# Delta-rule attention followed by two feed-forward layers, on one core: a new timetable for the start of the first layer and another order of its second matrix product

## The chip, the cores and the metric

The program is one kernel on one NeuronCore of a Trainium2 chip. What counts is the device time of one execution in microseconds (us), the median of several runs. The kernel's engines are TensorE (PE, with its weight loads PEld), VectorE (DVE), ScalarE (ACT), GpSimd (POOL) and SyncE (SP, which issues most transfers). A tile framework records the program in the order in which the Python code runs and sets the semaphores; each engine works off its own instructions in that order.

## The reference

Three stages run one after the other. The attention is a recurrence over 768 steps for 4 x 8 heads of width 48; the first feed-forward layer has 2048 hidden columns and a leaky activation with one slope for each column; the second has 1536 and a gated activation. The weights come out of the set-up as float64, since float32 arrays are multiplied there by a numpy float64.

```python
k_n = k / (np.linalg.norm(k, axis=-1, keepdims=True) + 1e-06)
for t in range(S):                      # attention: q, k, v, beta, S = 768
    y[:, :, t] = np.einsum('bhd,bhde->bhe', q[:, :, t], state)
    v_old = np.einsum('bhde,bhd->bhe', state, kt)
    state = state + bt[:, :, :, None] * np.einsum('bhd,bhe->bhde', kt, vt - v_old)
...
h = x @ w_in                            # first layer: x is 3072 x 384, w_in 384 x 2048
g = np.maximum(h, 0.0) + alpha * np.minimum(h, 0.0)
x = g @ w_out                           # back to 3072 x 384
...
g = x @ w_gate                          # second layer: 384 x 1536
out = (g * (1.0 / (1.0 + np.exp(-g))) * (x @ w_val)) @ w_out
```

## The kernel before

**The work.** The attention goes in 24 chunks of 32 steps; 4 chunks make a window. For each window the chunk's triangular system is inverted: `pre_T` transposes k or q on TensorE, `pre_G` makes the products of the keys, and `lanes` (windows 1 to 5) or `lanes2` (window 0, by blocks) does the substitution, a long row of small VectorE instructions (lines 258 and 266) with a part of the columns on GpSimd. Its last steps turn the result over into the tile TT (line 208). For each chunk there follow `do_KS` (keys times state, then `v` minus that on VectorE), `do_QS`, `do_U` (TT times v), `do_S` (the new state), `do_Y` and `do_XT` (the output, transposed into `xh` and `xl`, the high and the low part of x).

The first layer goes over 12 blocks of 256 tokens (two chunks) and 16 hidden slices: `H1(n, j)` is nine matmuls of 256 columns (line 600), then ScalarE (lines 610, 611) and VectorE (line 613) make the activation `pn`; `H1_parts` splits it into a high part `gh[0]` (ScalarE, line 621) and a low part `gh[1]` (GpSimd, line 622); `O1(n, j)` is nine matmuls with both (line 633). The second layer (`H2`, `O2`, lines 692 and 721) goes over 8 blocks of 384 tokens and 12 slices.

**Weights.** A matrix is used as a high and a low part, three products for each. The float64 words of a slice are turned into float32 by ScalarE (line 519) and three VectorE instructions (lines 527, 529, 533) and split by ScalarE (540) and GpSimd or VectorE (541). The generator `conv` does this for the 32 slices of the first layer, three steps a slice and 97 in all; `go(conv, n)` runs n steps of it. For the second layer the 36 slices are converted early, stored, fetched again at the end of the first layer (`fetch_w2`) and split (`make_w2`); 32 of them take the places of the first layer's slices.

**What sets the order.** `prelude()` is written out by hand. Everything after it stands in a list of events, each with a due time u; the list is sorted by u and run. One u is one pair of H1 and O1: `H1(n, j)` is due at 16n + j, `O1(n, j)` 2.5 later. The events of a chunk are due from `base(c)` on, here 20 for chunk 4, 25.7 for chunk 5, otherwise 8(c - 2). The first substitution on this list, window 1 (chunks 4 to 7), is spread over u = 6.6 to 18.5, the remaining 55 steps of `conv` over u = -0.5 to 13.5. `E1` is 192, the u at which the first layer's H1 ends.

Of the kernel before, what the change touches and what calls it, by code (L numbers as in the profile page):

```python
# [24 lines left out]
def kernel(  # L25
# [33 lines left out]
    NK = DM // 128  # L59
# [33 lines left out]
    nat = [ap.tile([128, H, 2, 64], F32, name=f"nat{z}") for z in range(2)]  # L93
# [207 lines left out]
    LANES = 5 + C - 1 + 1  # L301
# [286 lines left out]
    PASSES = ((0, 0), (0, 1), (1, 0))  # L588
# [36 lines left out]
    def O1(n, j):  # L625
        if j == 0:
            o1_t[n] = ps_o1.tile([128, 2, 512], F32, name="o1", tag="o1")
        o = o1_t[n]
        w = w1[2 * j + 1]
        g = g1_t.pop((n, j))  # L630
        for dm in range(NK):
            for i, (a, b) in enumerate(PASSES):
                nc.tensor.matmul(  # L633
                    o[:, dm // 2, (dm % 2) * N1:(dm % 2) * N1 + N1],
                    w[:, a, dm * 128:dm * 128 + 128],
                    g[:, b],
                    start=(j == 0 and i == 0 and dm % 2 == 0),
                    stop=(j == J1 - 1 and i == 2),
                    skip_group_check=True,
                )  # L640
        if j == J1 - 1:
            xs = g1.tile([128, 2, NK, 128], F32, name="xs", tag="xs", bufs=1)
            nc.scalar.activation(
                out=xs[:, :, 0:2, :].rearrange("p c k t -> p k c t"),
                in_=o[:, 0].rearrange("p (k c t) -> p k c t", k=2, c=2),
                func=AF.Copy,
            )
            nc.vector.tensor_copy(xs[:, :, 2, :], o[:, 1, 0:N1].rearrange("p (c t) -> p c t", c=2))
            nc.sync.dma_start(out=x2d[n], in_=xs)
            o1_t.pop(n)  # L650
# [87 lines left out]


    events = []  # L740

    def at(u, fn, *args):
        events.append((u, len(events), fn, args))
# [35 lines left out]
    conv = all_w1()  # L779

    def go(g, n=1):
        for _ in range(n):
            next(g, None)
# [4 lines left out]
    def prelude():  # L788
# [21 lines left out]
        n = 0  # L810
# [15 lines left out]
        inv = lanes2(0, True)  # L826
        go(inv, 3)
        n = 0
# [19 lines left out]
        warm(6)  # L848
        go(inv, 7)
        go(inv)  # L850
        go(conv, 4)
        go(inv)
        go(conv, 3)
        do_QS(0)
        do_U(0)
        go(conv, 3)
        do_S(0)
        load_k2(1)
        load_v(2)
# [4 lines left out]
        do_Y(0)  # L864
        do_QS(1)
        do_U(1)
        go(conv, 3)
        do_XT(0)
        go(conv, 2)
        do_Y(1)  # L870
# [3 lines left out]
        load_w1(*range(24, 2 * J1))  # L874
        go(conv, 3)
        do_XT(1)
        go(conv, 3)
        go(inv)
        go(conv, 3)
        go(inv)  # L880
        for z in range(4):
            pre_T(1, "q", z // 2, z % 2, nat)
        go(conv, 3)

    def base(c):
        return {4: 20, 5: 25.7}.get(c, 8 * (c - 2))

    CONV_DONE, CONV_END = 42, 14.0
    CONV_N = 3 * 2 * J1 + 1 - CONV_DONE
    for i in range(CONV_N):  # L890
        at(-0.5 + i * CONV_END / CONV_N, go, conv)
# [1 line left out]
    for w in range(1, NWIN):  # L893
        P = base(4 * w) - 32
        if w == 1:
            for z in range(2):
                at(0.6 + z, pre_G, 2 + z, (1,))
            for z in range(4):
                at(2.6 + z, pre_G, 4 + z)
            l0, l1, n = 6.6, 18.5, LANES  # L900
        else:
            at(P - 5, load_nat, w, "k", nat)
            at(P - 1, load_beta, w)
            for z in range(4):
                at(P + 1.2 + z, pre_T, w, "k", z // 2, z % 2, nat)
            at(P + 4.5, load_nat, w, "q", nat)
            for z in range(4):
                at(P + 7.2 + z, pre_T, w, "q", z // 2, z % 2, nat)
            for z in range(4):
                at(P + 11.2 + z, pre_G, 4 * w + z)  # L910
            l0, l1, n = P + 15, P + 31.5, LANES
        box = {}

        def step(w=w, box=box):
            if "g" not in box:
                box["g"] = lanes(w, 10)
            next(box["g"], None)

        for z in range(n):
            at(l0 + (l1 - l0) * z / n, step)  # L920

    for c in range(2, NCH):
        u = base(c)
        if c > 2:
            at(u - 7, load_v, c)
            at(u - 1.3, load_k2, c)
        at(u - 1.5, scale_v, c)
        at(u + 0.3, do_KS, c)
        at(u + 0.35, do_QS, c)
        at(u + 2.3, do_U, c)  # L930
        at(u + 4.3, do_S, c)
        at(u + 4.35, do_Y, c)
        at(u + 6.3, do_XT, c)
    for n in range(NB1):
        for j in range(J1):
            at(16 * n + j, H1, n, j)
# [2 lines left out]
    if WIDE2:  # L939
# [6 lines left out]
        for i in range(NW2):  # L946
            u = 24 + i * 4.0
# [5 lines left out]
    E1 = 16 * NB1  # L953
# [13 lines left out]
    late = list(range(2 * J1, 3 * J2))  # L967
    early2 = list(range(0, min(2 * J1, 3 * J2)))
    for i in early2:
        at(E1 - 16 + 1 + i / 2, fetch_w2, i)  # L970
        at(E1 - 16 + 3.1 + i / 2, make_w2, i)
    for i in late:
        at(E1 - 16 + 3 + i / 2, fetch_w2, i)
        at(E1 - 16 + 5.1 + i / 2, make_w2, i)
    at(E1 + LA + 0.6, end1)
    for n in range(NB2):
        u = E1 + LA + 1 + J2 * n
# [4 lines left out]
            at(u + j + 1.5, O2, n, j)  # L982

    with tc.manual_schedule():
        prelude()
        for _, _, fn, args in sorted(events, key=lambda e: e[:2]):
            fn(*args)

# [29 lines left out]
```

## Time and profile before

| what | value |
|---|---|
| median of 3 runs | 1161.68 us (1161.34 to 1162.38) |
| the profiled execution, its own time | 1160.9 us |
| its span, first to last instruction | 1159.2 us |
| mean granted TensorE clock | 0.953 |
| busy: TensorE, VectorE, ScalarE, GpSimd | 93%, 54%, 39%, 29% |

Outside the span lie 1.7 us of the profiled execution, and the median of the runs is 0.8 us above it. The busy shares are means over stages: up to about 76 us the attention of two chunks and the conversion alone, up to 696 us the first layer with the attention beside it, then the second layer. TensorE's granted clock stands at one of two levels, 1.0 (2.4 GHz) or 0.5 (1.2 GHz); a number between them is a mean over both. A figure such as "x163" is a count of instructions.

### The profile page before, as it was taken

Reading aid. Unit: us, or ns where it says so; the run is one execution under the profiler, and the core shown is the slowest. Engines: PE = TensorE matmul, PEld = TensorE weight load, DVE = VectorE, ACT = ScalarE, POOL = GpSimd, SP = SyncE. Lnnn points to the kernel's source line nnn. Section 1 sums busy time; section 2 is a strip of 40 time slices with the busy share of each in tenths; the row PEclk is TensorE's granted clock in tenths of the full one; section 3 lists DMA queues with packets and bytes.
Section 4 is the critical chain, followed back from the end, with each engine's and each line's share of the span. In section 5 each row is a group of like instructions: output and inputs, shape, how many; then the busy total and the mean of one; then the engine's idle time right before and its main releaser. Section 6 shows DMA issues by size and latency. Waiting matters only on the chain.

```text
span 1159.2 us, 37229 instructions
## 1 busy us (share of the span) xinstructions
PE 1083.7 (93%) x16125; PEld 1048.2 (90%) x16125; DVE 621.3 (54%) x1308; ACT 446.7 (39%) x1158; POOL 338.8 (29%) x522
## 2 busy tenths in 40 slices
PE   6578789899999999999999989999999999999996
PEld 5468689889989998998999979999999999999996
DVE  5669963794497379449734364333333333333332
ACT  4346344345435444544454673222222222222221
POOL 4234742563283256327433361101010000101000
PEclk8569789899999999999999999999999999999998
DMA  9652021234234323422322252010101010100000
GB/s 220 193 188 44 2 69 41 74 85 125 57 89 109 82 73 85 124 59 71 91 65 77 76 171 68 1 41 1 42 1 41 1 42 3 39 11 32 12 10 21
DMA packets 140080, 76.44 MB, mean 66 GB/s; under 512 B 104000, under 2 KB 134624, under 8 KB 139916
## 3 DMA queue, kind: packets, MB, share of 16 engines
q1 hardware_dynamic: 139340, 73.45, 23.3%
q8 instruction: 126, 2.06, 0.7%
q0 software_dynamic: 576, 0.61, 0.2%
q14 instruction: 38, 0.31, 0.1%
HBM read 57.52 MB, written 16.52 MB: 64 GB/s over the span
## 4 chain that ended last, share of the span: by engine, by line
PE 64%; DVE 17%; issue 13%; POOL 3%; ACT 2%; DMA 1%; POOLq 0%; SPq 0%; DVEq 0%; ACTq 0%
PE gv L692 21%; PE o L633 12%; PE h L600 11%; PE o L721 10%; DVE tmp L258 3%; DVE pn L613 2%; DVE X L266 2%; POOL w L541 2%; PE pg L168 2%; DVE wf L533 2%; PE pst L445 2%; PE pt L149 1%; DVE wf L529 1%; PE pu L427 1%; PE py L466 1%
## 5 line engine op out<-in xcount | busy, mean ns | idle before, releaser
L692 PE MATMUL gv<-x2s,w 128*128 128x384 f32 x1728 | 317.6, 336 | 0.0
L692 PEld LDWEIGHTS gv<-x2s,w 128*128 128x128 f32 x1728 | 304.1, 188 | 0.0
L633 PE MATMUL o<-gh,w 128*128 128x256 f32 x1728 | 256.2, 292 | 17.9 <-POOL gh L622 10.2
L600 PE MATMUL h<-xh,w 128*128 128x256 f32 x1152 | 242.9, 287 | 7.8 <-ACT pn L611 5.3
L633 PEld LDWEIGHTS o<-gh,w 128*128 128x128 f32 x1728 | 222.2, 193 | 29.8 <-POOL gh L622 14.8
L622 POOL TENSOR_TENSOR gh<-pn,gh 128x256 fp32r<-128x256 f32 x192 | 152.4, 794 | 304.2 <-ACT gh L621 255.3
L613 DVE SCALAR_TENSOR_TENSOR pn<-pn,nalpha 128x256 f32<-128x256 f32 x192 | 105.9, 551 | 186.8 <-ACT pn L611 182.7
L600 PEld LDWEIGHTS h<-xh,w 128*128 128x128 f32 x1152 | 195.3, 194 | 10.3 <-ACT pn L611 6.0
L600 PE MATMUL h<-xl,w 128*128 128x256 f32 x576 | 164.5, 286 | 2.0 <-DVE xl L492 2.0
L721 PE MATMUL o<-w,us 128*128 128x384 f32 x864 | 165.3, 336 | 0.0
L721 PEld LDWEIGHTS o<-w,us 128*128 128x128 f32 x864 | 151.1, 188 | 0.0
L704 DVE TENSOR_TENSOR sg<-sg,gv 128x384 f32<-128x384 f32 x96 | 53.2, 554 | 175.9 <-ACT sg L702 175.9
L621 ACT ACTIVATE gh<-pn 128x256 fp32r<-128x256 f32 x192 | 80.0, 416 | 141.8 <-DVE pn L613 141.3
L677 POOL TENSOR_TENSOR x2s<-x2r,x2s 128x384 fp32r<-128x384 f32 x21 | 20.7, 1014 | 333.8 <-ACT x2s L675 333.8
L600 PEld LDWEIGHTS h<-xl,w 128*128 128x128 f32 x576 | 111.8, 194 | 2.6 <-DVE xl L492 2.6
L707 ACT ACTIVATE us<-u 128x384 fp32r<-128x384 f32 x96 | 50.5, 526 | 165.0 <-DVE u L705 165.0
L610 ACT ACTIVATE pn<-h 128x256 f32<-128x256 f32 x192 | 72.2, 376 | 105.9 <-PE h L600 104.4
L702 ACT ACTIVATE sg<-gv 128x384 f32<-128x384 f32 x96 | 47.1, 491 | 169.4 <-PE gv L692 169.4
L708 DVE TENSOR_TENSOR us<-u,us 128x384 fp32r<-128x384 f32 x96 | 53.7, 559 | 62.8 <-ACT us L707 62.8
L705 DVE TENSOR_TENSOR u<-sg,gv 128x384 f32<-128x384 f32 x96 | 53.2, 554 | 45.8 <-PE gv L692 45.6
L611 ACT ACTIVATE pn<-h 128x256 f32<-128x256 f32 x192 | 72.5, 378 | 0.0
L258 DVE TENSOR_TENSOR tmp<-L,X 128x31 f32<-128x31 f32 (+29 forms) x155 | 64.2, 414 | 1.4
(102 smaller groups left out, 1062.3 us busy)
## 6 DMA issues: line engine op xcount, KB each, us to landing
w<-in_moe_w_out_dram SPq DMA_DIRECT2D x28, 384.0 KB
w2d<-wf SPq DMA_DIRECT2D x36, 192.0 KB
wf<-w2d SPq DMA_DIRECT2D x36, 192.0 KB
w<-in_moe_w_in_dram SPq DMA_DIRECT2D x16, 384.0 KB
nat<-in_k_dram SPq DMA_DIRECT2D x24, 192.0 KB
k<-in_k_dram SPq DMA_DIRECT2D x96, 48.0 KB
x2d<-xs SPq DMA_DIRECT2D x12, 384.0 KB
w<-in_moe_w_gate_dram SPq DMA_DIRECT2D x12, 384.0 KB
```

The costliest lines, as they stand in the source:

```text
L258: eng.tensor_tensor(w, t.L[:, i + 1:C, i:i + 1].to_broadcast([128, n, m]), t.X[:, i:i + 1, c0:c0 + m].to_broadcast([128, n, m]), ALU.mult,)
L600: nc.tensor.matmul(ps[:, 0:N1], w[:, a, kk * 128:kk * 128 + 128], x[b][:, kk, :], start=(i == 0), stop=(i == 3 * NK - 1),)
L610: nc.scalar.activation(out=pn[:, 1], in_=hv, func=AF.Relu, scale=-1.0)
L611: nc.scalar.activation(out=pn[:, 0], in_=hv, func=AF.Relu)
L613: nc.vector.scalar_tensor_tensor(out=g, in0=pn[:, 1], scalar=nalpha[:, j:j + 1], in1=pn[:, 0], op0=ALU.mult, op1=ALU.add)
L621: nc.scalar.activation(out=gh[:, 0], in_=g, func=AF.Copy)
L622: nc.gpsimd.tensor_tensor(gh[:, 1], g, gh[:, 0], ALU.subtract)
L633: nc.tensor.matmul(o[:, dm // 2, (dm % 2) * N1:(dm % 2) * N1 + N1], w[:, a, dm * 128:dm * 128 + 128], g[:, b], start=(j == 0 and i == 0 an ...
L692: nc.tensor.matmul(p[:, 0:N2], w2[j, z][:, a, kk * 128:kk * 128 + 128], x[:, b, kk], start=(i == 0), stop=(i == 3 * NK - 1),)
L704: nc.vector.tensor_tensor(sg, sg, ps[0], ALU.mult)
L708: nc.vector.tensor_tensor(us[:, 1], u, us[:, 0], ALU.subtract)
L721: nc.tensor.matmul(o2_t[n][t][:, 0:DM], us[:, a, t * 128:t * 128 + 128], w[:, b, :], start=(j == 0 and i == 0), stop=(j == J2 - 1 and i == 2),
```

## The change

Five things change.

- `O1` walks the three products in the outer loop and the three column blocks in the inner one, and the product with the low part of `gh` comes last: six matmuls now precede the first that reads `gh[1]`; before, one did.
- The prelude runs 39 steps of `conv` (before 42) with more of them ahead of chunk 1, and no longer holds the last two steps of window 0's substitution and the four transpositions of window 1's q; these are events now, due at u = -0.4 and 0.7 and at 3.6 to 6.6.
- The remaining 58 steps of `conv` stand between u = -0.5 and 11.0; the products of window 1's keys between 7.6 and 10.6; window 1's substitution between 11.8 and 23.6.
- Chunks 4 and 5 start at 22.6 and 27.2, and their steps after KS are 1.2 apart where the others have 2.
- The fetches and splits of the second layer's weights are 0.75 apart (before 0.5), so that 18 of the 36 splits are due after E1 (before: 10).

```diff
-        for dm in range(NK):
-            for i, (a, b) in enumerate(PASSES):
+        for i, (a, b) in enumerate(((0, 0), (1, 0), (0, 1))):
+            for dm in range(NK):
                 nc.tensor.matmul(
...
+        go(conv, 5)
+        go(inv)
         go(conv, 4)
-        go(inv)
-        go(conv, 3)
         do_QS(0)
         do_U(0)
-        go(conv, 3)
+        go(conv, 5)
         do_S(0)
...
         do_U(1)
-        go(conv, 3)
+        go(conv, 5)
         do_XT(0)
...
         do_XT(1)
-        go(conv, 3)
-        go(inv)
-        go(conv, 3)
-        go(inv)
-        for z in range(4):
-            pre_T(1, "q", z // 2, z % 2, nat)
-        go(conv, 3)
+        return inv
...
-        return {4: 20, 5: 25.7}.get(c, 8 * (c - 2))
+        return {4: 22.6, 5: 27.2}.get(c, 8 * (c - 2))
-    CONV_DONE, CONV_END = 42, 14.0
+    CONV_DONE, CONV_END = 39, 11.5
...
             for z in range(2):
                 at(0.6 + z, pre_G, 2 + z, (1,))
+            for z in range(2):
+                at(-0.4 + 1.1 * z, lambda: go(inv0[0]))
             for z in range(4):
-                at(2.6 + z, pre_G, 4 + z)
-            l0, l1, n = 6.6, 18.5, LANES
+                at(3.6 + z, pre_T, 1, "q", z // 2, z % 2, nat)
+            for z in range(4):
+                at(7.6 + z, pre_G, 4 + z)
+            l0, l1, n = 11.8, 23.6, LANES
...
+        f = 0.6 if c in (4, 5) else 1.0
-        at(u + 2.3, do_U, c)
-        at(u + 4.3, do_S, c)
-        at(u + 4.35, do_Y, c)
-        at(u + 6.3, do_XT, c)
+        at(u + 0.3 + 2 * f, do_U, c)
+        at(u + 0.3 + 4 * f, do_S, c)
+        at(u + 0.35 + 4 * f, do_Y, c)
+        at(u + 0.3 + 6 * f, do_XT, c)
...
     for i in early2:
-        at(E1 - 16 + 1 + i / 2, fetch_w2, i)
-        at(E1 - 16 + 3.1 + i / 2, make_w2, i)
+        at(E1 - 16 + 1 + i * 0.75, fetch_w2, i)
+        at(E1 - 16 + 3.1 + i * 0.75, make_w2, i)
     for i in late:
-        at(E1 - 16 + 3 + i / 2, fetch_w2, i)
-        at(E1 - 16 + 5.1 + i / 2, make_w2, i)
+        at(E1 - 16 + 1 + i * 0.75, fetch_w2, i)
+        at(E1 - 16 + 3.1 + i * 0.75, make_w2, i)
```

**First place: TensorE at the end of the prelude.** The rows start with the new state of chunk 1 (`pst`) and the transposition of its output (`px`). The products `pi` are the last two steps of window 0's substitution, `pt` the transpositions of window 1's q, and `h_1337` is the first H1. Before:

```order
L445 MATMUL pst<-U,k_105 64x48 x32
L488 MATMUL px<-ident,ys 128x128 x3
L343 MATMUL pi<-TT,GL 32x16 x64
L365 MATMUL pi<-tmp,Dm 32x16 x64
L149 MATMUL pt<-ident,nat_103 128x128 x8
L149 MATMUL pt<-ident,nat_104 128x128 x8
L600 MATMUL h_1337<-xh,w 128x256
```

Now, from the first `pi` on; `h_1236` is the first H1, `pk` and `py` are KS and QS of chunk 2, `pg` is its product of keys and queries:

```order
L343 MATMUL pi<-TT,GL 32x16 x64
L600 MATMUL h_1236<-xh,w 128x256
L600 MATMUL h_1236<-xl,w 128x256
L600 MATMUL h_1236<-xh,w 128x256 x2
L600 MATMUL h_1236<-xl,w 128x256
L600 MATMUL h_1236<-xh,w 128x256 x2
L600 MATMUL h_1236<-xl,w 128x256
L600 MATMUL h_1236<-xh,w 128x256
L401 MATMUL pk<-St,kqt 32x48 x32
L401 MATMUL py<-St,kqt 32x48 x32
L168 MATMUL pg<-kqt 32x32 x32
L365 MATMUL pi<-tmp,Dm 32x16 x64
```

The second product `pi` has moved behind the first H1 and the start of chunk 2, directly ahead of the second H1; the four groups `pt` have left this place (they stand behind the fourth to seventh H1 now).

**Second place: VectorE within window 1's substitution.** `tmp` and `X` are the substitution, `wf` and `we` the conversion, `w` a split, `pn` the activation of an H1. Before:

```order
L613 SCALAR_TENSOR_TENSOR pn<-pn,nalpha 128x256
L258 TENSOR_TENSOR tmp<-L,X 128x175
L266 TENSOR_TENSOR X<-X,tmp 128x25x7
L527 TENSOR_SCALAR we<-wf 128x384
L529 SCALAR_TENSOR_TENSOR wf<-wf,we 128x384
L258 TENSOR_TENSOR tmp<-L,X 128x192
L266 TENSOR_TENSOR X<-X,tmp 128x24x8
L533 SCALAR_TENSOR_TENSOR wf<-w_135,wf 128x384
L258 TENSOR_TENSOR tmp<-L,X 128x207
L266 TENSOR_TENSOR X<-X,tmp 128x23x9
L527 TENSOR_SCALAR we<-wf 128x384
L613 SCALAR_TENSOR_TENSOR pn<-pn,nalpha 128x256
```

Now:

```order
L613 SCALAR_TENSOR_TENSOR pn<-pn,nalpha 128x256
L258 TENSOR_TENSOR tmp<-L,X 128x175
L266 TENSOR_TENSOR X<-X,tmp 128x25x7
L258 TENSOR_TENSOR tmp<-L,X 128x192
L266 TENSOR_TENSOR X<-X,tmp 128x24x8
L258 TENSOR_TENSOR tmp<-L,X 128x207
L266 TENSOR_TENSOR X<-X,tmp 128x23x9
L613 SCALAR_TENSOR_TENSOR pn<-pn,nalpha 128x256
```

Between two activations the conversion's instructions have gone; they all stand ahead of the substitution now.

**Third place: TensorE where block 2 begins.** `px` is the transposition of chunk 5, `h_3667` the first H1 of block 2, which reads what is made of `px`. Before:

```order
L600 MATMUL h_3619<-xh,w 128x256
L633 MATMUL o_2733<-gh,w 128x256 x9
L488 MATMUL px<-ident,ys 128x128 x3
L600 MATMUL h_3667<-xh,w 128x256
L600 MATMUL h_3667<-xl,w 128x256
```

Now:

```order
L600 MATMUL h_3619<-xh,w 128x256
L488 MATMUL px<-ident,ys 128x128 x3
L633 MATMUL o_2690<-gh,w 128x256 x9
L600 MATMUL h_3667<-xh,w 128x256
L600 MATMUL h_3667<-xl,w 128x256
```

One O1 has changed places with the transposition and stands between it and the H1 that needs it.

## Rows read from the trace of the kernel before

**Rows 1.** Stretches of the span: length, busy time of each engine, PEclk, DMA share.

```profile
81.50:110.00 28.50, 27.52 (x784) 25.55 (x783) 26.69 (x51) 18.23 (x48) 14.45 (x14) 1.00 0.24 46
110.00:164.00 54.00, 39.45 (x397) 35.43 (x397) 51.59 (x125) 21.65 (x61) 32.00 (x59) 0.75 0.03 9
164.00:207.50 43.50, 43.48 (x1144) 40.79 (x1142) 16.09 (x31) 20.20 (x59) 12.19 (x16) 1.00 0.31 69
207.50:217.50 10.00, 6.38 (x147) 5.79 (x148) 6.19 (x13) 2.13 (x6) 2.90 (x4) 0.66 0.28 67
...
697.60:1151.50 453.90, 451.12 (x2588) 450.78 (x2587) 165.79 (x299) 116.04 (x236) 25.54 (x26) 1.00 0.07 22
```

**Rows 2.** Timeline of TensorE, 61 to 82 us: start, duration, what.

```profile
61.67 0.40 PE L343 MATMUL pi<-TT,GL 32*32 32x16 f32 x13
64.22 1.78 PE L343 MATMUL pi<-TT,GL 32*32 32x16 f32 x115 [2.16 <-issue]
66.48 0.40 PE L365 MATMUL pi<-tmp,Dm 16*32 16x16 f32 x13 [0.47 <-ACT tmp L358]
69.05 1.78 PE L365 MATMUL pi<-tmp,Dm 16*32 16x16 f32 x115 [2.17 <-issue]
...
76.27 0.56 PE L600 MATMUL h<-xh,w 128*128 128x256 f32 x1
...
78.47 1.47 PE L401 MATMUL pk<-St,kqt 48*32 48x48 f32 x64
...
81.12 0.39 PE L600 MATMUL h<-xh,w 128*128 128x256 f32 x1
```

**Rows 3.** Timeline of VectorE at the first activation.

```profile
80.83 0.78 DVE L613 SCALAR_TENSOR_TENSOR pn<-pn,nalpha 128x256 f32<-128x256 f32 x1 [7.01 <-ACT pn L611]
```

**Rows 4.** VectorE's groups by line, 81.5 to 164 us: busy us, mean ns.

```profile
L533 DVE SCALAR_TENSOR_TENSOR wf<-w,wf 128x384 int32<-128x384 int32 x18 | 13.2, 735 | 0.1
...
L613 DVE SCALAR_TENSOR_TENSOR pn<-pn,nalpha 128x256 f32<-128x256 f32 x20 | 12.3, 615 | 8.3 <-ACT pn L611 8.2
L529 DVE SCALAR_TENSOR_TENSOR wf<-wf,we 128x384 int32<-128x384 int32 x17 | 11.3, 665 | 0.1
...
L527 DVE TENSOR_SCALAR we<-wf 128x384 int32<-128x384 int32 x17 | 7.1, 417 | 0.0
...
L181 DVE TENSOR_TENSOR mt<-pg,mask 128x256 f32<-128x256 f32 x6 | 2.5, 415 | 0.6 <-ACT GL L178 0.6
```

**Rows 5.** TensorE in one stretch, matmuls of line 600 alone (x: count).

```profile
0.00:176.40 176.40, 36.07 (x216) 32.09 (x217) 0.76 0.45 118
```

**Rows 6.** Timelines of VectorE and of TensorE after the substitution.

```profile
162.80 1.11 DVE L208 STREAM_TRANSPOSE TT<-X 128x512 f32<-128x512 f32 x1
...
176.48 0.28 PE L600 MATMUL h<-xh,w 128*128 128x256 f32 x1
```

**Rows 7.** Timeline of TensorE at the start of block 2.

```profile
206.99 0.49 PE L488 MATMUL px<-ident,ys 128*128 128x128 f32 x3
209.30 0.44 PE L600 MATMUL h<-xh,w 128*128 128x256 f32 x1 [1.82 <-ACT xh L491]
211.56 0.58 PE L600 MATMUL h<-xl,w 128*128 128x256 f32 x1 [1.81 <-DVE xl L492]
...
216.28 1.32 PE L633 MATMUL o<-gh,w 128*128 128x256 f32 x9
```

**Rows 8.** Waits of TensorE, 164 to 672 us: sum, times, longest.

```profile
PE o L633 <- POOL gh L622: 3.9, 9, 0.6
```

**Rows 9.** Stretches at the end of the first layer, columns as in Rows 1.

```profile
653.00:671.75 18.75, 18.75 (x163) 18.75 (x162) 8.39 (x15) 13.31 (x37) 9.85 (x12) 1.00 0.55 165
671.75:688.74 16.99, 15.33 (x120) 14.17 (x118) 11.36 (x16) 12.67 (x36) 11.28 (x13) 1.00 0.53 158
688.74:696.27 7.53, 5.54 (x30) 4.53 (x29) 5.03 (x6) 4.79 (x13) 5.91 (x7) 0.86 0.52 155
```

**Rows 10.** Timeline of VectorE in the last block.

```profile
675.71 1.01 DVE L613 SCALAR_TENSOR_TENSOR pn<-pn,nalpha 128x256 f32<-128x256 f32 x1 [1.04 <-ACT pn L611]
```

More of the change, by code (lines that the diff above doesn't have):

```diff
@@ L740 @@
     events = []
+    inv0 = []
     def at(u, fn, *args):
@@ L984 @@
     with tc.manual_schedule():
-        prelude()
+        inv0.append(prelude())
         for _, _, fn, args in sorted(events, key=lambda e: e[:2]):
```

## The prediction

> **What bounds the kernel now.** I read the stretches first, then the timelines inside the ones that aren't full. From 697.6 us on, the second layer, TensorE is busy 451.1 of 453.9 us [rows 1]: nothing is to be had there. From 164 to 207.5 us it is busy without a gap at full clock, with VectorE at 37%: bound by TensorE. From 81.5 to 164 us it is the other way round: VectorE is busy 26.7 of 28.5 and 51.6 of 54.0 us, TensorE in the second part only 39.5 of 54, at a mean clock of 0.75 [rows 1]. There VectorE is the limit. It has the conversion of the weights, window 1's substitution and the activations in one queue, and TensorE waits for the activations behind them. Three smaller losses stand in the timelines: the stretch before 81.5 us, where TensorE does what no H1 needs while VectorE idles for 7 us [rows 2, 3]; the start of block 2, where the first H1 waits twice [rows 7]; and the end of the first layer, where the last 24.5 us hold more than their matmuls [rows 9].
>
> So the change is to be judged by one question: VectorE's work is the same, but how far has TensorE got when VectorE is through with it?
>
> **Start.** TensorE goes from the transposition of chunk 1 straight to a product of the substitution, 61.67 to 66.00 us, with a pause of 2.16 us for which the profile shows no releaser. Then now come the first H1, as before 2.20 us (76.27 to 78.47), the three small products 2.65 us (78.47 to 81.12), and the second product of the substitution, 4.35 us with its pause (66.48 to 70.83) [rows 2]. I add 0.5 us, an estimate, for VectorE's subtraction that frees the buffer of the second H1. That H1 starts at 66.00 + 2.20 + 2.65 + 4.35 + 0.5 = 75.7 instead of 81.12 us. Its activation follows 2.2 us of matmuls and the 2.4 us that lay between the first H1's end and its activation (78.47 to 80.83 [rows 2, 3]): 80.3 us. That gap can be shorter by about 1.5 us if ScalarE is free; I take 79.5. The four transpositions taken out here cost their time later, in the stretch where TensorE has idle time. The prelude does three steps of conversion fewer in all but more of them ahead of chunk 1; they lie in VectorE's idle time there if it is as long as the 7.0 us of [rows 3], and cost up to 0.7 us each (the mean of line 533 [rows 4]) where it is not.
>
> **VectorE's stretch.** I counted what stands in VectorE's order from the second activation to the last transposition of the substitution, line 208, and set it against what the trace has from 81.5 us to that instruction's end at 163.9 us [rows 6]. All counts agree but five: 23 activations for 20, and one each fewer of lines 533, 529, 527 and 181. With the means of [rows 4] that is 3 x 0.615 less 0.735 + 0.665 + 0.417 + 0.415: 0.4 us less. So 82.0 us from 79.5: line 208 ends at 161.5 us, only 2.4 us earlier than before.
>
> The gain is in what TensorE has done by then. Its U of chunk 4, the first to need the result, now stands behind the 25th H1. Before, 24 H1 (216 matmuls) were done by 176.4 us [rows 5] and the 25th ran from 176.48 us [rows 6]; with nine matmuls of 0.115 us (18.75 us for 163 [rows 9]) it ended at 177.5. Now that point is at 161.8, 15.7 us earlier, if TensorE keeps up. It needs for this: 67 us busy in the two parts before, about 10 less at full clock throughout (a mean of 0.75 over 54 us is 27 us at the low level, so half of the 39.5 us ran at half speed), 10 more for five more pairs of H1 and O1, 3 for transpositions and chunk 4's first steps: 70 of 82 us. At the low level for t us it can do 82 - t/2, so it keeps up while t is under 24 us. Before it was 27. I take off 3 us for this and for waits on single activations, and 0.8 for U of chunk 4, which lay before that point and now lies behind it: **11.9 us**. The ends: 15 if the clock holds, 4 if the start gains nothing and the clock falls more often. The shorter steps of chunks 4 and 5 still leave an H1 or an O1 and often both between two steps, 1 to 2 us; that is as long as one of the waits of [rows 7].
>
> **Start of block 2.** The first H1 waited 1.82 us for xh and 1.81 for xl [rows 7]. Now an O1 of 1.05 us stands between, and xl stands ahead of the second turnover of the next substitution in VectorE's queue where it was behind it and behind its small steps. I keep 0.5 of 3.6 us. The waits also dropped the clock: 0.66 over 10 us [rows 1] is 6.8 us at half, in which the 4.7 us from 211.56 to 216.28 would take about 2.4. Together 3.1 + 2.4 = **5.5 us**; the ends are 1.5 (the O1 alone hides its length) and 6.
>
> **O1's order.** From 164 to 672 us TensorE waited 9 times for the low part, 3.9 us, at most 0.6 [rows 8]. Six matmuls of 0.115 us take 0.7 where one took 0.1, so these waits are covered. But they stand where VectorE is late with the activations, and TensorE may reach the next such wait earlier only to wait longer: I take **2.5 us**, between 1 and 5.5 (all of it, and some of the low clock that goes with it).
>
> **End of the first layer.** From 671.75 to 696.27 us there are 16 groups of nine matmuls, 16.7 us at 0.115; 24.5 were taken, so 7.8 are lost [rows 9]. The low part comes late there because the weights' splits go through the same three engines: an activation takes 1.01 us on VectorE [rows 10] where the mean was 0.62 [rows 4]. With splits 0.75 apart there are 1.33 for each pair instead of 2, and the low part is read last. I take **6.5 us**, between 3.5 and 7.8. The splits that move into the second layer lie beside a full TensorE with VectorE at 37% and ScalarE at 26% [rows 1]; if one were late there, TensorE would wait for all of it.
>
> A rule of the Trainium skill bears on this (SBUF — State Buffer, section "Who interferes with whom"): a VectorE instruction with two inputs in SBUF and a GpSimd instruction that reads SBUF exclude each other, the later one waits for all of the earlier. The 1.01 us agrees with that. By the rule the splits on GpSimd go on holding up activations, only less often, and the term would be nearer its lower end, which makes the sum 3 us smaller.
>
> **Sum.** 11.9 + 5.5 + 2.5 + 6.5 = 26.4 us from the profiled execution's 1160.9 is 1134.5; the median of the runs stood 0.8 above it: **1135 us**.
>
> **Rivals.**
>
> *The clock eats a part of the gain.* In VectorE's stretch TensorE waits a little in each pair, and it was such a stretch that had the mean of 0.75. If half of the new stretch runs at the low level, the 70 us of work take T with T - T/4 = 70, so 93 us instead of 82 + 3: 8 us more, 1143. Against it: before, TensorE was at full clock from 81.5 to 110 us with VectorE nearly full, and the idle per pair is now smaller than in the second part. Chance 0.15. The Trainium skill speaks for this rival (TensorE: Matmul & The Clock Gate, section "HAM oscillation — how this bites in real kernels"): waits between bursts bring the low clock back, and the cost is paid at each. The 0.75 agrees.
>
> *Slower.* The same place, further on: all of the gain is gone when that stretch takes 82 + 3 + 26 = 111 us, and with 70 us of work this needs 83 us at the low level, three quarters of it; 1164 and more from there on. Against it: a TensorE at half speed is the limit and so without waits, and [rows 1] have no stretch as low. Chance 0.04, with 0.02 for ending near no change.
>
> *The start doesn't move.* The added conversion holds up chunks 0 and 1, or the pauses without a releaser grow; then the 25th H1 comes 4 us later: 1139. Chance 0.15.
>
> *The splits wait in the other layer.* If the end gains nothing, or gives it back as waits in the second layer: 6.5 us, 1142. Chance 0.08.
>
> That leaves 0.56 for the forecast. Its own range is 1129 to 1141, from about 6 us of error in its terms; with the rivals 1127 to 1150. Faster by over 0.2% (about what this measurement can tell from no change): 0.94; within it 0.02; slower 0.04.
>
> **What would show it.** The second H1 at about 76 us; line 208 of window 1 ending near 161 to 165 us with the 25th H1 done; VectorE still nearly full up to there; a mean clock of 0.8 or more in that stretch; the first H1 of block 2 without a wait over 1 us, near 195 us; waits for the low part under 1 us in sum after 164 us; the last first-layer matmul some 17 us after the tenth H1 of the last block; the second layer still within 452 us. It is wrong if VectorE's stretch gets longer than 86 us or TensorE's idle time moves behind it, to chunks 4 and 5.

## The result, and the profile after

| | before | after |
|---|---|---|
| median of the runs | 1161.51 us (1160.03 to 1162.38, 4 runs) | 1149.65 us (1146.89 to 1151.53, 4 runs) |
| ratio to before | | 0.9897, 95% interval 0.9873 to 0.9921 |
| the profiled execution, its span | 1160.9, 1159.2 us | 1151.5, 1149.8 us |
| mean granted clock | 0.953 | 0.968 |

The change made the kernel 11.9 us faster. The forecast was 26.4; the time lies in the forecast's range, at its upper end, and outside the likeliest case's own (1129 to 1141). The profiled execution of after is the slowest of its four, so the two traces differ by 9.4 us.

**The start.** TensorE's timeline in the kernel after (start, duration, what; in brackets the idle time before it and its releaser), the answer to [rows 2]; "x" counts rows of the trace, two for each of the small products:

```profile
62.99 0.90 PE L488 MATMUL px<-ident,ys 128*128 128x128 f32 x3
63.82 0.40 PE L343 MATMUL pi<-TT,GL 32*32 32x16 f32 x13
66.38 1.78 PE L343 MATMUL pi<-TT,GL 32*32 32x16 f32 x115 [2.16 <-issue]
68.09 0.58 PE L600 MATMUL h<-xh,w 128*128 128x256 f32 x1
69.20 0.58 PE L600 MATMUL h<-xl,w 128*128 128x256 f32 x1 [0.54 <-DVE xl L492]
...
71.21 1.51 PE L401 MATMUL pk<-St,kqt 48*32 48x48 f32 x64
72.50 1.39 PE L401 MATMUL py<-St,kqt 48*32 48x48 f32 x64
73.72 0.23 PE L168 MATMUL pg<-kqt 48*32 48x32 f32 x4
76.57 0.80 PE L168 MATMUL pg<-kqt 48*32 48x32 f32 x60 [2.63 <-issue]
77.30 1.14 PE L365 MATMUL pi<-tmp,Dm 16*32 16x16 f32 x68
81.95 1.04 PE L365 MATMUL pi<-tmp,Dm 16*32 16x16 f32 x60 [3.50 <-issue]
82.91 0.58 PE L600 MATMUL h<-xh,w 128*128 128x256 f32 x1
```

The first H1 starts at 68.09 (before 76.27), the second at 82.91: not at the 75.7 of the prediction, and 1.8 us later than before. Two pauses without a releaser stand ahead of it, 2.63 and 3.50 us, and between the two lie 60 + 68 rows, 128 in all.

**VectorE's stretch.** VectorE's timeline, the second activation and the end of the substitution (the answer to [rows 3, 6]):

```profile
85.93 0.48 DVE L613 SCALAR_TENSOR_TENSOR pn<-pn,nalpha 128x256 f32<-128x256 f32 x1 [2.01 <-ACT pn L611]
...
174.52 1.05 DVE L208 STREAM_TRANSPOSE TT<-X 128x512 f32<-128x512 f32 x1
```

So 89.6 us lie between the second `pn` and the end of line 208 (prediction: 82.0, from 79.5 to 161.5). VectorE's groups in this stretch (busy us, mean ns, idle time before them), against [rows 4]:

```profile
L613 DVE SCALAR_TENSOR_TENSOR pn<-pn,nalpha 128x256 f32<-128x256 f32 x23 | 13.3, 577 | 6.5 <-ACT pn L611 6.4
...
L533 DVE SCALAR_TENSOR_TENSOR wf<-w,wf 128x384 int32<-128x384 int32 x17 | 12.3, 726 | 0.1
...
L529 DVE SCALAR_TENSOR_TENSOR wf<-wf,we 128x384 int32<-128x384 int32 x16 | 9.7, 606 | 0.8
L527 DVE TENSOR_SCALAR we<-wf 128x384 int32<-128x384 int32 x16 | 7.6, 472 | 0.0
```

The counts are those that the prediction set against [rows 4], but the stretch is 89.6 us, and 6.4 us of it are waits for ScalarE's part of the activation. The stretches (length, busy time of each engine, clock, DMA share), against [rows 1]:

```profile
85.90:112.00 26.10, 21.24 (x407) 19.39 (x398) 22.81 (x41) 17.33 (x46) 10.64 (x11) 0.97 0.24 46
112.00:175.60 63.60, 53.62 (x968) 49.69 (x960) 58.66 (x134) 28.39 (x85) 36.80 (x67) 0.95 0.15 34
```

TensorE's clock is 0.97 and 0.95 where it was 1.00 and 0.75; TensorE is busy 75 of the 90 us. Its matmuls of line 600 up to 176.5 us, against the 216 of [rows 5]:

```profile
0.00:176.50 176.50, 35.62 (x225) 31.16 (x225) 0.82 0.45 118
```

One H1 more, the 25th, at the point where the prediction wanted to be 15.7 us earlier.

**What ScalarE waits for** from 85.9 to 112 us (sum, times, longest):

```profile
ACT wf L519 <- POOL w L541: 4.1, 4, 2.1
ACT wf L519 <- DVE w L541: 2.4, 3, 0.9
ACT w L540 <- DVE wf L533: 2.0, 4, 0.8
```

All three are waits of the conversion, and lines 610 and 611 of the activation stand behind them in the same queue. The conversion held ScalarE as long before the change. From 84.2 to 110 us, where VectorE waited only 1.2 us for `pn` up to line 208, the kernel before has:

```profile
ACT wf L519 <- POOL w L541: 3.6, 5, 1.7
ACT w L540 <- DVE wf L533: 2.8, 6, 0.9
ACT wf L519 <- DVE w L541: 2.5, 2, 1.9
```

**The later places.** TensorE at the start of block 2, against [rows 7]:

```profile
208.63 0.49 PE L488 MATMUL px<-ident,ys 128*128 128x128 f32 x3
208.88 1.29 PE L633 MATMUL o<-gh,w 128*128 128x256 f32 x9
210.01 0.36 PE L600 MATMUL h<-xh,w 128*128 128x256 f32 x1
210.81 0.38 PE L600 MATMUL h<-xl,w 128*128 128x256 f32 x1 [0.44 <-DVE xl L492]
```

The wait of 1.82 us for `xh` is gone, that of 1.81 for `xl` has shrunk to 0.44. TensorE's waits from 164 to 672 us, against [rows 8]:

```profile
PE o L633 <- ACT gh L621: 5.8, 10, 1.2
PE py L466 <- issue: 4.2, 4, 1.2
PE pu L427 <- DVE v L414: 3.4, 4, 0.9
```

The 3.9 us for GpSimd's `gh` are gone; waits for the high part, for `v` and for no visible releaser stand there. The end of the last block, whose tenth H1 starts at 667.54 and whose last O1 ends at the first H2 (686.17), against [rows 9]:

```profile
667.30:681.50 14.20, 14.20 (x123) 14.16 (x122) 8.90 (x14) 10.40 (x30) 9.11 (x11) 1.00 0.40 114
681.50:686.20 4.70, 3.90 (x28) 3.26 (x27) 2.76 (x5) 3.83 (x11) 3.26 (x5) 1.00 0.35 114
```

**Where the 9.4 us came from.** U of chunk 4 and the 25th H1 were both done at 177.5 us before (where the prediction put them) and at 176.9 after: 0.6 us. The second H1 of block 2 starts at 214.60 (before 217.4): 2.2 more. The first H1 of the last block starts at 648.6 (652.9): 1.4 more. The first H2 starts at 686.2 (696.1): 5.7 more. The second layer gives back 0.5.

### The profile page after: what moved, and what is told of

The parts are those of the page before. It is cut to its first block, busy times and chain, and to the rows that moved or that the text cites. A ratio compares the mean times of both kernels' runs of the same rounds, so it can differ in the third digit from the quotient of the medians.

```text
span 1149.8 us, 37236 instructions
## 1 busy us (share of the span) xinstructions
PE 1072.2 (93%) x16125; PEld 1037.8 (90%) x16125; DVE 621.0 (54%) x1308; ACT 444.9 (39%) x1158; POOL 340.6 (30%) x522
## 4 chain that ended last, share of the span: by engine, by line
PE 63%; DVE 13%; issue 10%; ACT 1%; DMA 1%; POOL 0%; POOLq 0%; DVEq 0%; ACTq 0%; SPq 0%
PE gv L692 22%; PE o L633 12%; PE h L600 11%; PE o L721 10%; DVE tmp L258 4%; DVE pn L613 3%; DVE X L266 2%; PE pg L168 1%; PE pst L445 1%; PE py L466 1%; PE pt L149 1%; PE pu L427 1%; PE pk L401 1%; DVE wf L533 1%; PE py L401 1%
## 5 line engine op out<-in xcount | busy, mean ns | idle before, releaser
L633 PE MATMUL o<-gh,w 128*128 128x256 f32 x1728 | 249.4, 289 | 11.6 <-ACT gh L621 7.8
L600 PE MATMUL h<-xh,w 128*128 128x256 f32 x1152 | 239.2, 284 | 0.8 <-ACT pn L611 0.8
L633 PEld LDWEIGHTS o<-gh,w 128*128 128x128 f32 x1728 | 218.1, 190 | 21.5 <-ACT gh L621 10.8
L613 DVE SCALAR_TENSOR_TENSOR pn<-pn,nalpha 128x256 f32<-128x256 f32 x192 | 102.3, 533 | 174.6 <-ACT pn L611 171.7
L600 PEld LDWEIGHTS h<-xh,w 128*128 128x128 f32 x1152 | 191.8, 190 | 2.9 <-ACT pn L611 1.5
L541 POOL TENSOR_TENSOR w<-wf,w 128x384 fp32r<-128x384 f32 x42 | 45.7, 1090 | 80.7 <-ACT w L540 80.7
```

What stands on the lines that cost most here:

```text
L600: nc.tensor.matmul(ps[:, 0:N1], w[:, a, kk * 128:kk * 128 + 128], x[b][:, kk, :], start=(i == 0), stop=(i == 3 * NK - 1),)
L613: nc.vector.scalar_tensor_tensor(out=g, in0=pn[:, 1], scalar=nalpha[:, j:j + 1], in1=pn[:, 0], op0=ALU.mult, op1=ALU.add)
L633: nc.tensor.matmul(o[:, dm // 2, (dm % 2) * N1:(dm % 2) * N1 + N1], w[:, a, dm * 128:dm * 128 + 128], g[:, b], start=(j == 0 and i == 0 an ...
```

## The experiments

Two theories. **Theory 1**: the second H1 is late because of TensorE's pauses, and the transfers of the weights (`load_w1`) make the pauses long. A pause is idle time for which the profile shows no releaser ("issue"). **Theory 2**: VectorE idles because ScalarE's queue is held by the conversion ahead of the activations. Rivals: the parts of the change hinder one another; the stretch is VectorE's work and nothing else; the added conversion in the prelude holds up chunk 1. All ratios are to the kernel before, on the same chip; gains in us are the ratios' distances from 1 times 1161.5.

### The parts alone

O1's order alone in the kernel before:

```diff
-        for dm in range(NK):
-            for i, (a, b) in enumerate(PASSES):
+        for i, (a, b) in enumerate(((0, 0), (1, 0), (0, 1))):
+            for dm in range(NK):
```

> The kernel before with O1's new order alone: the product with the low part last. By the prediction's term, the 3.9 us in which TensorE waited for the low part between 164 and 672 us go, and some of the low clock with them: 2.5 us faster, 1 to 5.5, and a little more at the end of the first layer. The rival: TensorE only reaches the next wait, for the high part or for the activation, earlier and waits there longer; then under 1 us, and single waits of about 1 us stand on ScalarE's gh and VectorE's pn where those on GpSimd's gh stood.

Measured: 0.9983 (0.9967 to 0.9998), 2.0 us faster. The size of the term, no more than that: its interval goes from 0.2 to 3.8 us and so includes the rival's "under 1".

The splits' spacing alone (`i / 2` to `i * 0.75` in the four lines, as in the change):

> The kernel before with the wider spacing of the second layer's splits alone. By the prediction most of the 6.5 us at the end of the first layer comes from this: 3.5 to 6.5 us faster, the first H2 as much earlier, the second layer as long as before. The rival: the loss at the end is that of the low part in O1, and the spacing without O1's order gives under 2 us, or the late splits wait in the second layer and it gives nothing.

Measured: 0.9966 (0.9953 to 0.9980), 3.9 us faster. In the trace the last block takes 38.3 us from its first H1 to the first H2, before 43.2: 4.9 us. O1's order alone has 41.8 there, so 1.4; the whole change 37.5, so 5.7. The spacing does most of it.

The timetable alone (the change without these two):

> The kernel before with the timetable of the start alone (prelude, events of conversion and window 1, chunks 4 and 5), O1 and the splits as before. The traces of before and after differ by 1.0 us at the point where the 25th H1 and U of chunk 4 are done and by 2.8 at the second H1 of block 2. If the timetable made these alone: 2 to 4 us faster. If the timetable needs O1's order (its stretch has O1 wait for the low part too), under 1 us or slower. The prediction's two terms for it were 17.4.

Measured: 0.9937 (0.9915 to 0.9960), 7.3 us faster, 4.6 to 9.9. Both expectations were too low; they came from the profiled execution of after. That one has a stretch of low clock (0.5) at 176.05 to 179.46 us, which the trace of this run doesn't have: here 32.1 us lie between the end of line 208 and the first H1 of block 2, there 34.4. Of these 2.3 us, 0.8 are a pause that is 0.98 us there and 0.21 here. The parts give 13.2 us together and the whole 11.9: they don't hinder one another within their intervals. The timetable is worth 7.3 of the 17.4 us that the prediction gave it. That is where most of the forecast went wrong. In this run too the second H1 is at 82.5 us and the stretch behind it 89.7 us long.

### The start

The loads of the last eight slices behind the second H1:

```diff
-        load_w1(*range(24, 2 * J1))
...
+    for i in range(24, 2 * J1):
+        at(1.2 + (i - 24) * 0.25, load_w1, i)
```

> The changed kernel with the loads of the last eight slices of the first layer's weights issued behind the second H1 and not in the prelude. Theory 1 (the pauses of TensorE for which no releaser is shown get longer where weight loads fill the DMA): the two pauses of 2.63 and 3.50 us before the second H1 shrink to about 1 us each, the second H1 starts at about 79.5 instead of 82.9, and the kernel gains 1 to 3.5 us, less if VectorE's stretch only takes it back. Rival: the pauses have their length from something else, they stay at 2.5 to 3.5, and the time moves by less than 1 us or gets worse through late weights.

Measured: 0.9879 (0.9853 to 0.9904), not to be told from the change's 0.9897. The pauses are 3.00 and 1.59 us, the second H1 is at 81.3. With the loads in place the timetable alone had 3.70 and 1.59, the change 2.63 and 3.50. So this size scatters from run to run by more than the loads move it: the second half of theory 1 is not shown. Of use is that the stretch behind is 89.7 us here as well, so that its end moves one for one with its start.

256 extra products on TensorE ahead of the second H1, all in one place:

```diff
+    def dummies():
+        for _ in range(256):
+            nc.tensor.matmul(warm_t[0][0:32, 0, 0:16], ident[0:32, 0:32], ident[0:32, 0:16], start=True, stop=True)
+    at(0.95, dummies)
```

> The changed kernel with 256 extra products of 32x16 on TensorE directly ahead of the second H1; their result is used nowhere. Theory 1 (the instructions of TensorE come in packets of 16 KB, one for 128 small matmuls with their weight loads, about 3.7 us apart at the least): two packets more, the second H1 6.5 to 8 us later than in the changed kernel (at 89.5 to 91 instead of 82.9), two more pauses among the products, and the kernel about as much slower. Rival (the products take what they take, 15 ns each at the low clock as the 115 in 1.78 us): 3.9 us later or less, without new pauses.

Measured: 1.0127 (1.0107 to 1.0147). Neither came: with all products in one place their 512 rows took 53 ns each, 27.4 us without one pause:

```profile
82.22 27.41 PE L886 MATMUL warm<-ident 32*32 32x16 f32 x511
109.56 0.58 PE L600 MATMUL h<-xh,w 128*128 128x256 f32 x1
```

In the trace's list of DMA packets, the packets of 16 KB on the queue named "instruction" start at 92.28, 99.15 and 105.98 us, 6.85 us apart; that is 128 rows of 53.5 ns. So one packet goes with 128 rows, and where these last 6.85 us nothing waits. This run also tells what a late second H1 costs: it came 26.7 us later than in the change, line 208 ended 26.7 later, and the kernel was 26.7 slower by the ratios.

128 extra products, placed as those of the substitution are:

```diff
+        for y in range(32):
+            for b in range(4):
+                r = slice(32 * b, 32 * b + 16)
+                nc.tensor.matmul(
+                    warm_t[0][r, 0, 16 * (y % 16):16 * (y % 16) + 16],
+                    ident[r, 0:16], ident[r, 0:16], start=True, stop=True, skip_group_check=True,
+                )
```

> The changed kernel with 128 extra products of 16x16 ahead of the second H1, placed on TensorE's rows and columns as those of the substitution are (256 rows of the trace); their result is used nowhere. In the run with 256 products in one place each row took 53 ns, one instruction packet of 16 KB came every 6.85 us, so for each 128 rows, and no pause was left. Here the rows are short: by theory 1 the packets come 3.6 to 3.9 us apart, the rows take 15 ns and the rest is pauses, and the second H1 moves by 7.2 to 7.8 us. Rival: only the rows' own time, 256 at 15 ns, 3.9 us.

Measured: 0.9943 (0.9917 to 0.9968). TensorE's timeline:

```profile
74.61 0.72 PE L168 MATMUL pg<-kqt 48*32 48x32 f32 x60 [1.53 <-issue]
75.26 0.76 PE L365 MATMUL pi<-tmp,Dm 16*32 16x16 f32 x68
78.88 0.98 PE L365 MATMUL pi<-tmp,Dm 16*32 16x16 f32 x58 [2.86 <-issue]
...
79.72 0.78 PE L888 MATMUL warm<-ident 16*16 16x16 f32 x64
82.61 1.26 PE L888 MATMUL warm<-ident 16*16 16x16 f32 x128 [2.11 <-issue]
86.34 0.70 PE L888 MATMUL warm<-ident 16*16 16x16 f32 x60 [2.47 <-issue]
86.97 0.58 PE L600 MATMUL h<-xh,w 128*128 128x256 f32 x1
```

The pauses end at 74.61, 78.88, 82.61 and 86.34: 4.27, 3.73 and 3.73 us apart, each time 128 rows, and a packet of 16 KB starts 2.2 to 2.7 us ahead of each of these ends. From the last `pi` to the second H1 it is 7.3 us (79.70 to 86.97), 4.6 of them in two new pauses. Theory 1 without the loads holds: short rows come no faster here than 128 in about 3.7 us. The start alone could not have told: against the change's profiled run the second H1 is 4.1 us later, which is what the rival had (3.9). The two new pauses tell, and the 256 rows took some 2.7 us and not 3.9. The pauses ahead of the extra products add up to 4.4 us here and to 6.1 in the change, 1.7 less, and such sizes scatter. The kernel was 5.3 us slower by the ratios.

The last step of window 0's substitution behind the second H1:

```diff
-                at(-0.4 + 1.1 * z, lambda: go(inv0[0]))
+                at(-0.4 + 1.6 * z, lambda: go(inv0[0]))
```

> The changed kernel with the last step of window 0's substitution (64 products, one of the places of a pause) moved behind the second H1, where VectorE has its next work by then. In the changed kernel, in the one with the timetable alone and in the one with late loads the time from the second activation pn to the end of line 208 was 89.7 us, so what the second H1 gains should come out at the end one for one. Theory 1, as the last runs left it (a pause comes with every 128 small matmuls, an instruction packet of 16 KB starts about 2.5 us ahead of its end, loads only add to that): the second H1 goes ahead of one pause and of the 64 products, 3 to 4.5 us earlier, and the kernel is 2 to 4 us faster. Rival: the stretch behind it grows by as much, since VectorE or the substitution's end is late elsewhere; under 1 us.

Measured: 0.9866 (0.9832 to 0.9900), a median 3.7 us under the change's; the intervals overlap, so the trace has to say it: the second H1 at 79.7 (3.2 earlier), the end of line 208 at 173.5 (2.1 earlier). As theory 1 expected, less 1.1 us that the stretch took back.

The prelude's conversion as before, 33 steps ahead of the transposition of chunk 1, and `CONV_DONE` 33 (`go(conv, 5)`, `4` and twice `5` back to `4`, `3` and twice `3`):

> The changed kernel with the prelude's conversion as before, 33 steps up to the transposition of chunk 1 and not 39; the six steps stand in the events. If the added steps hold up chunks 0 and 1 (a rival of the prediction): the transposition at 60.8 to 61.2 instead of 63.0 us, the second H1 about 2 us earlier, and VectorE's stretch behind it longer by the work of six steps, 4 to 5 us, so that the kernel ends 2 to 3 us slower than the changed one. If the pauses alone moved the start: the transposition stays at 62.5 to 63.

Measured: 0.9933 (0.9889 to 0.9977), 4 us slower than the change by the ratios, though the intervals overlap. The transposition is at 60.9 us, the second H1 at 80.3, and the stretch 95.1 us long. The transposition's place at 62.99 in the profiled run of the change is not the added steps alone: in five other runs with the same prelude it is at 61.3 to 62.7, in the kernel before and the two with a part of the change at 60.8 to 61.6. The means are 62.0 and 61.1, so by an estimate from these nine runs the added steps cost about 0.9 us there; the rest scatters.

### VectorE's stretch

The conversion loosened: line 519 one slice ahead and not two, the split a step later.

```diff
-        for i in range(-2, n + 1):
-            if i + 2 < n:
-                w1_s[i + 2].act()
+        for i in range(-1, n + 1):
+            if i + 1 < n:
+                w1_s[i + 1].act()
...
-                if z == 0 and i > 0:
+                if z == 1 and i > 0:
...
-                if z == 1 and rest:
+                if z == 2 and rest:
                     rest()
-                if i < n or z == 1:
+                if i < n or z == 2:
```

> The changed kernel with the conversion's order loosened: ScalarE's line 519 one slice ahead and not two, the split one step later, so that neither waits for what VectorE or GpSimd have only just been given. Theory 2 (ScalarE's queue is held by the conversion, and the activations stand behind it): VectorE's wait for pn from 86 to 110 us falls from 6.4 to about 2 us, the 89.7 us from the second pn to the end of line 208 fall to 84 to 87, and the kernel gains 2.5 to 5 us. Rival: VectorE's work alone sets the stretch, or TensorE's H1 are what is late; the stretch stays at 88 to 90 and the time within 1 us.

Measured: 0.9840 (0.9802 to 0.9879), a median of 1144.2 us. The second `pn` is at 83.19 and line 208 ends at 169.7: 86.5 us, 3.1 less. Its waits from 83.1 to 109.3 us, VectorE's and then ScalarE's:

```profile
DVE pn L613 <- ACT pn L611: 2.0, 1, 2.0
```

```profile
ACT w L540 <- DVE wf L533: 4.9, 6, 1.8
ACT gh L621 <- DVE pn L613: 1.5, 2, 0.9
ACT pn L610 <- PE h L600: 0.8, 2, 0.6
```

Line 519 no longer waits, and over the whole stretch VectorE's idle time for `pn` is 3.1 instead of 6.4 us. All of its idle time there is 4.5 instead of 8.2 us, while its busy time grew from 81.5 to 82.1. Theory 2 holds for that part of the excess: 3.7 us of idle time, 3.1 of 7.6 us net. The profiled execution gained more than theory 2 says (span 1142.5 against 1149.8): the second H1 also came 2.7 us earlier, and the low clock at 176 us is absent. Of the 2.7, 1.6 lie ahead of the transposition of chunk 1 (61.34 us, where five runs with the tighter order have 61.3 to 62.7) and 1.1 in shorter pauses; how much of it the looser order makes can't be told from the scatter.

The same in the kernel before:

> The kernel before with the same loosened conversion. There VectorE was idle only about 4 of the 82.5 us of its stretch, though ScalarE waited as much for the conversion. Theory 2: the control moves little, 0 to 2 us faster. Rival (the conversion holds up the kernel before as well): as much as in the changed one, 2.5 to 5.

Measured: 0.9981 (0.9966 to 0.9996), 2.2 us faster, between theory 2's 0 to 2 and the rival's 2.5 to 5; the interval, 0.5 to 3.9, reaches into both. The trace speaks for theory 2, since the stretch got no shorter. The second H1 came 3.1 us earlier and the stretch behind took most of it back (from the second `pn` to line 208 81.6 us, before 79.7).

### Together

Late loads, moved step and loosened conversion, the edits as above:

> The changed kernel with the late loads, the moved step of the substitution and the loosened conversion together. If the two theories hold and add up: the second H1 4 to 5 us earlier, the stretch 3 to 5 us shorter, 6 to 9 us faster than the changed kernel, about 0.983 of the kernel before. If the gains meet the same limit (TensorE, which has 75 us of work in that stretch): 3 to 5 us.

Measured: 0.9827 (0.9796 to 0.9859), a median of 1142.1 us, 7.5 under the change's: the fastest kernel of the study, though not to be told from the loosened conversion alone. The second H1 is at 75.5 us, where the prediction had wanted it, but the third only at 82.5, behind the moved products and a pause of 1.63 us, and the stretch from the second `pn` is 89.7 us again. Line 208 ends at 168.3, only 1.4 us ahead of the loosened conversion alone: the gains do not add up.

The same with all low parts of the weights on GpSimd (`W1_DVE = 32`, before 16):

> The kernel with late loads, moved step and loosened conversion, and all low parts of the first layer's weights on GpSimd (now eight of them, 6.0 us in the stretch, are VectorE's). If VectorE's own work sets what is left of its stretch (82.4 us busy of 89.8 there): the stretch 3 to 6 us shorter, the kernel as much faster, 1136 to 1139. Rival: GpSimd, with 1.1 us for each, holds up the ring of the conversion or the low parts of the activations, or TensorE's 75 us are the limit; within 1.5 us or slower.

Measured: 0.9843 (0.9827 to 0.9860): no gain. But VectorE's busy time in the stretch did not fall (82.9 us, without this edit 82.4), so the run doesn't tell whether VectorE's work sets what is left of the stretch; that stays open. Its groups from 78 to 115 us without this edit, GpSimd's split last:

```profile
L529 DVE SCALAR_TENSOR_TENSOR wf<-wf,we 128x384 int32<-128x384 int32 x12 | 9.0, 752 | 0.6
L533 DVE SCALAR_TENSOR_TENSOR wf<-w,wf 128x384 int32<-128x384 int32 x13 | 8.0, 614 | 0.2
L527 DVE TENSOR_SCALAR we<-wf 128x384 int32<-128x384 int32 x12 | 7.0, 585 | 0.0
...
L541 POOL TENSOR_TENSOR w<-wf,w 128x384 fp32r<-128x384 f32 x7 | 7.9, 1133 | 5.2 <-ACT w L540 3.2 <-PE px L488 2.0
```

and with it:

```profile
L529 DVE SCALAR_TENSOR_TENSOR wf<-wf,we 128x384 int32<-128x384 int32 x13 | 12.1, 930 | 0.8
L533 DVE SCALAR_TENSOR_TENSOR wf<-w,wf 128x384 int32<-128x384 int32 x12 | 8.5, 712 | 0.2
L527 DVE TENSOR_SCALAR we<-wf 128x384 int32<-128x384 int32 x13 | 8.1, 621 | 0.0
...
L541 POOL TENSOR_TENSOR w<-wf,w 128x384 fp32r<-128x384 f32 x13 | 15.0, 1162 | 7.8 <-ACT w L540 7.6
```

VectorE lost six splits (3.8 us), and the three lines of the conversion took 4.7 us more, on 38 instructions for 37.

## Why the prediction was wrong

**The start: the step that failed first.** "That H1 starts at 75.7": it started at 82.9, 7.2 us later. The sum had the products in the right order and one pause, 2.17 us inside the 4.35. But [rows 2] show 115 and 13 rows between one pause and the next, 128. In the new order a boundary falls within `pg` and the next within `pi`, both ahead of the second H1 and behind rows too short to cover it: 6.1 us instead of 2.2. Counting the rows would have given the second one. Another 2.1 us come from the first H1 at 68.09 instead of 66.00: px is 2.15 us later, of which the rival "the start doesn't move" (added conversion) explains about 0.9. The other 1.1 us are small terms: the first H1 took 0.9 us more than 2.20 (0.54 of it a wait for `xl`) and the products between 0.8 more than 2.65, while the 0.5 us for VectorE's subtraction did not show. The rival named both causes and came true in kind; its price, 4 us, was too low, since the second `pn` is 6.4 us later than forecast.

**VectorE's stretch: the second.** "So 82.0 us": it was 89.6 to 89.7 in the change, with the timetable alone, with the late loads and with the 128 extra products. The count of instructions was right; the idle time was taken over from the trace of before, 4.2 us. It became 8.2: 4.0 us more. The runs show 3.7 of these as the conversion's order. ScalarE waited as long for the conversion before the change (8.9 us, now 8.5), so that alone doesn't make VectorE idle. That the steps of the substitution, which stood between the activations (the second excerpt of order), had filled VectorE's waits fits the order, but no run shows it. The other 3.6 us of the excess are longer busy time. The rows show it in several lines: line 258, with 31 instructions in both kernels, takes 12.7 us where it took 11.2, line 527 takes 7.6 for 16 where 17 took 7.1, and line 541 6.0 for 8 where it took 5.4. The last experiment shows that the conversion's instructions get longer when GpSimd has more of it, but what lengthened these lines in the change itself was not tried. The sentence "it is wrong if VectorE's stretch gets longer than 86 us" is what happened.

Together: U of chunk 4 was to be done 15.7 us earlier (161.8 against 177.5). The second `pn` took 6.4 of it (85.9 instead of 79.5), the stretch 7.6, U itself 1.0 more than the 0.3 it was given behind line 208 (to 176.9); 0.7 is left, the 0.6 above. TensorE was through with the 25th H1 at 173.7 us and waited for line 208, so the 3 us taken off for clock and waits weren't needed up to there.

**Start of block 2: mechanism right, size off in the profiled run.** 5.5 was forecast, 2.2 measured. The two waits went from 3.63 to 0.44 us as predicted. New pauses of 0.86 and 0.98 us (192.68 and 203.94 us) and the low clock from 176.05 took some of it back; the timetable alone, without that low clock and with pauses of 0.88 and 0.21 us, has 2.3 us more, 4.5.

**O1's order: as forecast, within a wide interval.** 2.5 forecast, 2.0 alone (0.2 to 3.8), 1.4 in the trace. The rival effect is there too: waits for the high part and for `v` take the place of a part of those for the low part.

**End of the first layer: right.** 6.5 forecast, 5.7 measured, inside 3.5 to 7.8. (The 16.7 us of its sum for 144 matmuls of 0.115 are 16.6, which changes nothing.) The stretch up to 681.5 us is full, 14.20 of 14.20 us. That the splits wait in the other layer did not happen: from the first H2 to the end it is 463.6 us, before 463.1.

**The clock** did not eat the gain (0.95 to 0.97 in the stretch, where the rival had 0.75). The oscillation that the Trainium skill describes (TensorE: Matmul & The Clock Gate, section "HAM oscillation — how this bites in real kernels") shows as single drops, at 131.7, 145.3 and 176.1 us, each behind a wait or a pause of 1.3 to 2.0 us, while a wait of 1.82 us up to 102.2 and the longest one, 2.99 us up to 157.4, have none behind them; so the trace agrees with it in part. The drop at 176.1 lasted 3.4 us at half speed, which by estimate cost up to 1.7 us of this trace; the traces of the other runs have none at this place. (In the rival "slower", 111 us with 70 us of work need 82 us at the low level, not 83.)

## What to carry to other kernels

Before moving small matmuls ahead of something urgent, count their rows from the last pause without a releaser: if the pauses recur at a fixed count, move short ones away from there (the moved step brought the second H1 3.2 us forward). Long rows had no pause in the run with 256 products, but putting long matmuls where a pause falls due was not tried as a gain. When work that interleaved two others is moved away, don't carry the old idle time over: ask what may have filled the waits, and read the waits of the in-order queue that feeds the bottleneck engine. And take a single trace's landmarks with their scatter: here one low-clock stretch and pauses of 1.5 to 3.9 us moved them by 2 to 3 us between runs of the same start.

## What the runs showed of the hardware

- TensorE's instructions come in packets of 16 KB, one for 128 rows of small matmuls. Where rows are short, the ends of two pauses are 3.7 us or more apart, and a packet starts 2.2 to 2.9 us before the end of a pause. The Trainium skill (Runtime: NRT & Kernel Launch, section "Instruction fetch mechanics") gives blocks of 16 KiB with 256 instructions, which agrees if each row's weight load counts as one, and says that the cost is mostly hidden; with short rows it isn't here: the two packets of the 128 extra products cost 2.1 and 2.5 us.
- Taking six splits off VectorE and giving them to GpSimd lengthened the conversion on VectorE: line 529 from 752 to 930 ns, line 533 from 614 to 712. The Trainium skill (SBUF — State Buffer, section "Who interferes with whom") has VectorE instructions with two inputs in SBUF exclude GpSimd's reads; both lines have two, and the numbers agree with it in kind. Line 527 with one input grew less, from 585 to 621.
